# Joining the two head tiles in the second mix, and re-timing softmax, spare banks and fillers around both ends of a two-mix kernel

## The chip, the cores and the metric

One NeuronCore of a Trainium2 chip runs the whole program. The metric is device microseconds of one execution; lower is better. The profile's times count from the span's start.

## The reference

Three layers follow each other over a batch of 2 sequences of 4160 tokens, 192 channels wide, in float32 (five of the weights arrive as float64):

```python
# 1. attention over a window of 7 tokens, 8 heads
w = softmax(weight_gen, axis=-1)                       # (2, 4160, 8, 7)
x = einsum('bshk,bskhg->bshg', w, windows(x_pad))      # token s sees s-6 .. s
# 2. first mix: token shift, squared ReLU, sigmoid gate
xk = mu_k * x + (1 - mu_k) * x_prev;  xr = mu_r * x + (1 - mu_r) * x_prev
x = sigmoid(xr @ w_r) * (maximum(xk @ w_k, 0)**2 @ w_v)        # hidden width 1024
# 3. second mix: ReLU, convolution over 3 tokens, gate
h = maximum(x @ w_in, 0)                                       # hidden width 1024
x = (h * sigmoid(conv3(h, conv_w))) @ w_out
```

## The kernel before

The tokens of each sequence are cut into ten tiles (SIZES, line 16): 256, 248, seven of 472, and 352. Channels lie on partitions in both mixes, tokens along the free dimension.

**Attention** (`attention`, line 401) runs on GpSimd. A tile's rows are loaded from DRAM by SyncE; a tile has 2, 4 or 3 slots of 128 tokens per batch, and each slot of each batch (a "token" call, line 409) is four GpSimd instructions on `prod`, the last of which writes `tok`. Softmax weights sit in `sw`. `softmax` (line 371) computes them in six steps: VectorE's maximum over the window, a subtraction (GpSimd, for tile 0 VectorE), ScalarE's Exp, VectorE's sum, VectorE's reciprocal, a multiplication (GpSimd). It is done for tiles 0, 1, 2, and for tiles 3 to 9 as seven blocks whose maxima and sums lie in `stage`.

**Mixing** (`mixing`, line 430) transposes `tok` on TensorE into a `pa` bank (flip) and forms the shifted blends. It has three units per tile: unit 0 is batch 0's first 128 channels, unit 1 is batch 1's, unit 2 the last 64 channels of both. A value is kept as a rounded part and a remainder (`hi`, `lo`), so each product takes several passes. The remainder is GpSimd's work (VectorE's for tile 0). Unit 2's results are spread by DMAs into `xB`.

**First mix** (`moe1`, line 528): for each tile i, batch b and chunk fi of 128 of the 1024 hidden columns, five matmuls into a `pa` bank (two of them), two ScalarE steps (Relu, Square), a ScalarE copy and a VectorE subtraction into a buffer `s` (two), then five matmuls into the accumulators `am` and `ar`. `gate_r` (line 510) makes the gate, `mix_out` (line 587) multiplies it in and writes the next layer's input `x2[b]`; `carry` (line 575) keeps the last two columns of the tile before.

**Second mix** (`moe2`, line 623): for the same i, b, fi, five matmuls into a `pc` bank (two of them), Relu into `h` (two), a scaled copy back to the bank, two taps of the convolution (VectorE, line 645), Sigmoid, a product, a copy and a subtraction into `g` (two), and five matmuls into the accumulators `bm` and `br`. `store` (line 681) writes the outputs.

**Weight preparation** (`prepare`, line 351; `narrow`, line 286): SyncE loads chunks of the float64 weights into three slots of `stage`; `narrow` rebuilds float32 in two PSUM tiles px and py with one ScalarE and five VectorE steps. px alternates between `bm` and `br`, py between the two `pc` banks (lines 254 and 255). `split` makes the rounded part and the remainder.

**The order.** Every step is put on a plan at a program time t by `at(t, ...)`: tile i's first mix starts at 16 i, batch 1's half at 16 i + 8, one unit per chunk; the second mix follows LAG = 10 units later. Buffers rotate in plan order (`Ring`). `Program.schedule` (line 99) then orders each engine's instructions: a list scheduler with hand-fitted durations (`cost`, line 72) starts, on whichever engine is free first, the ready instruction with the smallest t. A PSUM tile counts as one region whatever columns are named (line 68). The resulting order is fixed; on the chip each engine runs its list in order and waits for semaphores. A result becomes ready for others after a latency; between two TensorE instructions there is none:

```python
for j in succ[i]:
    ready[j] = max(ready[j], t + dur[i] if eng == "PE" == self.ops[j][0] else end)
```

All DMAs are issued by SyncE in one such list.

Of the kernel before, what the change touches and what calls it, by code (L numbers as in the profile page):

```python
# [8 lines left out]
F32R = mybir.dt.float32r  # L9
# [17 lines left out]
LAG = 10  # L27

# [5 lines left out]
class Program:  # L34
# [37 lines left out]
    def cost(self, eng, method, out, ins, pointer):  # L72
# [21 lines left out]
        if eng == "POOL":  # L94
            busy = 0.1 + (n / 455 if method == "tensor_tensor" else n / 270)
            return busy, busy + 0.12
        return 0.6, 0.6

    def schedule(self):
# [42 lines left out]
        for _ in range(n):  # L142
# [22 lines left out]
        for i in sorted(range(n), key=lambda i: (start[i], i)):  # L165
            eng, method, a, k = self.ops[i][:4]
            getattr(self.real[eng], method)(*a, **k)  # L167
# [14 lines left out]
def conv_moe_kernel(ctx: ExitStack, tc: tile.TileContext, xp, wg_first, wg_rest, mus, w_k, w_v, w_r, w_in, conv_w, w_out, out):  # L182
# [18 lines left out]

    W = NMAX + 4

# [167 lines left out]
    def softmax(j, a, b, eng, times, bank):  # L371
# [19 lines left out]
        for t, fn in zip(times, (lambda: fold(m, ALU.max), lambda: each(m, ALU.subtract), s3,  # L391
                                 lambda: fold(z, ALU.add), s5, lambda: each(m, ALU.mult))):
            at(t, fn)
# [36 lines left out]
    def mixing(i, u, t, dt_):  # L430
        N, P, e = SIZES[i], PART[i], EXTRA[i]
        c = 1 if u == 2 else 0
        st = {}

        def flip():
            p = pa_r()
            st["p"] = p[:, e:e + N]
            st["q"] = p
            x = tok_t[i]
            k = (0, 256, 128)[u]  # L440
            for l in range(SLOTS[i]):
                PE.transpose(p[:, l:l + SLOTS[i] * (P - 1) + 1:SLOTS[i]], x[:, l, k:k + 128], ident)

        def shifted(fn):
            a = att_r()[:, :N]
            if e:
                fn(a, st["q"][:, e - 1:e + N - 1])
            else:
                POOL.memset(a[:, 0:1], 0.0)
                fn(a[:, 1:N], st["q"][:, 0:N - 1])  # L450
# [6 lines left out]
        def m1(k):  # L457
# [3 lines left out]
            if i < 2:  # L461
                a = shifted(lambda y, x: ACT.activation(y, x, ACTF.Copy, scale=onemu[:, own]))
                DVE.scalar_tensor_tensor(out=st[k][:, :N], in0=st["p"], scalar=mu[:, own], in1=a, op0=ALU.mult, op1=ALU.add)
            else:
                DVE.scalar_tensor_tensor(out=st[k][:, :N], in0=st["d"], scalar=onemu[:, own],
                                         in1=st["p"], op0=ALU.mult, op1=ALU.add)

        def hi(k):
# [6 lines left out]
            ACT.copy(x[:, 0, :N], st[k][:, :N])  # L475
# [351 lines left out]
```

## Time and profile before

| | us |
|---|---|
| median of 3 runs | 791.23 |
| lowest, highest | 789.27, 791.41 |
| profiled execution | 793.36 |
| its span | 791.6 |

Busy shares of the span: TensorE 88%, ScalarE 84%, VectorE 80%, GpSimd 64%. A share is an average over stretches with different limits; the rows below cut the span into stretches and then look at single engines. PE is TensorE's matmuls, PEld its weight loads, DVE VectorE, ACT ScalarE, POOL GpSimd, SP SyncE. Each row of a timeline gives start, duration, engine, line, operation, out<-in, shape and count; in square brackets stands the idle time before it and what ended it. Line 167 is the planner's call that issues everything.

### The profile page before, as it was taken

The numbers are of one execution on the slowest core, as the hardware profiler recorded it, in microseconds if no ns is written. First come the engines' busy times: TensorE is split into PE (matmuls) and PEld (weight loads), VectorE is DVE, ScalarE is ACT, GpSimd is POOL, SyncE is SP. The second block draws the span as 40 slices with busy tenths as digits, with TensorE's granted clock in tenths as the row PEclk, the third lists the DMA queues.
The fourth block names the chain that finished last, engine by engine and source line by source line (L and its number), as shares of the span: only waits on it lengthen the run. The fifth ranks groups of instructions, "written<-read, shape, count | busy, mean of one in ns | idle before, by whom it ended". The sixth has DMA issues, their size and how long they took to land.

```text
span 791.6 us, 10781 instructions
## 1 busy us (share of the span) xinstructions
PE 697.2 (88%) x3505; PEld 607.3 (77%) x3505; DVE 631.4 (80%) x1137; ACT 666.5 (84%) x1441; POOL 506.2 (64%) x368
## 2 busy tenths in 40 slices
PE   0066776999999999999999999999999999999964
PEld 0054675898888888888888888888888888889843
DVE  5987977887878787878877887879787878788764
ACT  2467798998989899989898989989898989899854
POOL 5898888899999999999999789295401101000000
PEclk9997786999999999999999999999999999999998
DMA  7685010130130112112121211020002000100000
GB/s 202 194 277 174 13 51 11 58 103 10 61 99 19 51 69 59 59 51 91 28 69 51 68 46 58 7 68 1 20 12 56 20 1 21 35 19 1 20 14 14
DMA packets 19241, 45.09 MB, mean 57 GB/s; under 512 B 3057, under 2 KB 14705, under 8 KB 19057
## 3 DMA queue, kind: packets, MB, share of 16 engines
q1 hardware_dynamic: 19184, 44.41, 18.9%
q8 instruction: 27, 0.44, 0.2%
q14 instruction: 30, 0.24, 0.1%
HBM read 27.40 MB, written 6.39 MB: 43 GB/s over the span
## 4 chain that ended last, share of the span: by engine, by line
PE 68%; ACT 15%; DVE 13%; issue 2%; DMA 2%; SPq 0%; ACTq 0%; DVEq 0%
PE pa L167 21%; PE pc L167 16%; PE am L167 10%; PE bm L167 9%; PE ar L167 7%; PE br L167 5%; DVE pc L167 4%; ACT pa L167 2%; ACT pc L167 2%; DVE stage L167 2%; ACT h L167 2%; ACT g L167 2%; ACT L167 1%; DMA stage<-in_moe_w_k_dram 1%; DVE bm L167 1%
## 5 line engine op out<-in xcount | busy, mean ns | idle before, releaser
L167 DVE SCALAR_TENSOR_TENSOR pc<-h,cw,pc 128x472 f32<-128x472 f32 (+3 forms) x320 | 208.1, 650 | 39.5 <-ACT pc L167 36.7
L167 POOL TENSOR_TENSOR prod<-rows,sw 128x1344 f32<-128x1344 f32 x70 | 216.1, 3087 | 12.8 <-DMA rows<-in_x_dram 7.8
L167 ACT ACTIVATE pa<-pa 128x472 f32<-128x472 f32 (+3 forms) x320 | 160.8, 505 | 39.1 <-PE pa L167 35.2
L167 POOL TENSOR_TENSOR prod<-prod 128x576 f32<-128x576 f32 (+1 forms) x140 | 171.0, 1221 | 8.6
L167 PE MATMUL bm<-g,wo 128*128 128x472 f32 (+3 forms) x480 | 148.7, 360 | 21.3 <-ACT g L167 21.1
L167 PE MATMUL am<-s,wv 128*128 128x472 f32 (+3 forms) x480 | 147.0, 367 | 7.1 <-ACT s L167 5.8
L167 DVE TENSOR_TENSOR pc<-h,pc 128x472 f32<-128x472 f32 (+3 forms) x160 | 94.7, 592 | 59.2 <-ACT pc L167 57.9
L167 PE MATMUL pa<-xA,wkA 128*128 128x472 f32 (+3 forms) x480 | 125.9, 368 | 7.5 <-DVE s L167 3.4
L167 PE MATMUL pc<-x,wiA 128*128 128x474 f32 (+3 forms) x480 | 121.6, 361 | 3.5 <-DVE g L167 3.5
L167 POOL TENSOR_TENSOR xA<-mk,xA 128x472 fp32r<-128x472 f32 (+2 forms) x36 | 40.4, 1128 | 123.1 <-ACT xA L167 96.6
L167 PE MATMUL ar<-s,wv 128*128 128x472 f32 (+3 forms) x320 | 112.6, 364 | 4.9 <-DVE x L167 3.3
L167 PEld LDWEIGHTS bm<-g,wo 128*128 128x128 f32 x480 | 88.3, 191 | 35.4 <-ACT g L167 26.0
L167 PE MATMUL br<-g,wo 128*128 128x472 f32 (+3 forms) x320 | 112.4, 355 | 1.4 <-DVE ob L167 1.4
L167 DVE TENSOR_TENSOR s<-pa,s 128x472 fp32r<-128x472 f32 (+3 forms) x160 | 93.7, 586 | 16.8 <-ACT s L167 15.8
L167 DVE TENSOR_TENSOR g<-pc,g 128x472 fp32r<-128x472 f32 (+3 forms) x160 | 93.8, 586 | 15.5 <-ACT g L167 14.0
L167 PEld LDWEIGHTS am<-s,wv 128*128 128x128 f32 x480 | 89.1, 197 | 21.4 <-ACT s L167 11.0
L167 PEld LDWEIGHTS pa<-xA,wkA 128*128 128x128 f32 x480 | 87.6, 199 | 19.9 <-DVE s L167 6.4
L167 ACT ACTIVATE pc<-h,cw 128x472 f32<-128x472 f32 (+3 forms) x160 | 99.7, 623 | 1.8
L167 PEld LDWEIGHTS pc<-x,wiA 128*128 128x128 f32 x480 | 85.7, 193 | 15.9 <-DVE g L167 5.8
L167 ACT ACTIVATE h<-pc 128x474 f32<-128x474 f32 (+3 forms) x160 | 84.4, 527 | 11.4 <-PE pc L167 8.3
L167 ACT ACTIVATE pc<-pc 128x472 f32<-128x472 f32 (+3 forms) x160 | 80.9, 506 | 14.0 <-DVE pc L167 13.0
L167 PE MATMUL pa<-xB,wkB 128*128 128x472 f32 (+3 forms) x320 | 89.8, 362 | 1.5 <-DMA xB<-mk 1.5
(105 smaller groups left out, 1066.4 us busy)
## 6 DMA issues: line engine op xcount, KB each, us to landing
rows<-in_x_dram SPq DMA_DIRECT2D x14, 960.0 KB, 4.5
xB<-rm SPq DMA_DIRECT2D x28, 118.0 KB, 2.3
xB<-mk SPq DMA_DIRECT2D x28, 118.0 KB, 2.3
out_dram<-om SPq DMA_DIRECT2D x14, 236.0 KB, 2.0
rows<-in_x_dram SPq DMA_DIRECT2D x4, 768.0 KB, 7.1
rows<-in_x_dram SPq DMA_DIRECT2D x2, 864.0 KB, 4.5
out_dram<-ob SPq DMA_DIRECT2D x14, 118.0 KB, 2.2
stage<-in_moe_w_v_dram SPq DMA_DIRECT2D x4, 384.0 KB, 3.9
```

Of the source, the lines that this page charges most:

```text
L167: getattr(self.real[eng], method)(*a, **k)
```

## The change

What it does, part by part:

- SIZES become 256, 220, seven of 476, 352. The first mix keeps ten tiles. In the second mix tiles 0 and 1 are one unit of 476 columns: `moe2` and `store` are planned for i >= 1 only, at tile 1's times, over `x2` columns that `mix_out` of both tiles has filled (OFFSET, UNIT).
- The planner treats a GpSimd result as ready for GpSimd when the instruction ends (as for TensorE), and its GpSimd durations change by 0.05 us.
- Softmax of tiles 3 to 9 moves from program times 16.5 to 25 (and 24.9 + 16 j for the last step) to 32.1 to 40 (and 36.1 + 12.5 j). Its seven Exps become one over all seven blocks, at 35.2. Its load may not be issued before planned time 50 us (40 before). Attention of tile 3 moves later by 2.4 (load) and 3.2 units.
- Weight preparation of the second mix moves from program times 4.4 to 10 to 6 to 18. px is `bm` alone, py `br` alone.
- Spare buffers are lent. Until program time 24 `moe1` and flips rotate over `pa` and `pc` banks, and `s` over `s` and `g` buffers. From 160.3 on `moe2` rotates over `pc` and `pa` banks, `h` over `h` and `mk`, `g` over `g` and `s`.
- Fillers: matmuls of 248 columns on a constant tile `spare`, into columns 264 to 511 of the `am` bank, which no one reads. The planner puts them in front of TensorE instructions before which it sees a gap over 0.3 us, until the first matmul that covers those columns (tile 2's). Within 9 us before the first matmul a gap gets 0.88 gap / 0.225 of them, later 0.65 gap / 0.12.
- First loads: SyncE issues tile 0's rows of batch 0, then `sw`, then `mu` (before: `mu`, `sw`, rows). A VectorE memset fills `spare`.
- A flip issues its transposes with the last slot first. (The diff also lets `mixing` take units 3 and 4; none is planned.)

```diff
-SIZES = [256, 248] + [472] * 7 + [352]
+SIZES = [256, 220] + [476] * 7 + [352]
+OFFSET = [0, SIZES[0]] + [0] * (NTILE - 2)
+UNIT = [None, SIZES[0] + SIZES[1]] + SIZES[2:]
+DONE = 16 * NTILE + 0.3
+LENT = 24
...
             for j in succ[i]:
-                ready[j] = max(ready[j], t + dur[i] if eng == "PE" == self.ops[j][0] else end)
+                ready[j] = max(ready[j], t + dur[i] if eng in ("PE", "POOL") and eng == self.ops[j][0] else end)
...
+            if eng == "PE":
+                idle &= not self.covers(a[0])
+                gap = start[i] - max(last, first - 9.0)
+                if idle and gap > 0.3:
+                    cold = start[i] <= first
+                    for _ in range(int((0.88 if cold else 0.65) * gap / (0.225 if cold else 0.12))):
+                        self.filler()
+                last = start[i] + dur[i]
             getattr(self.real[eng], method)(*a, **k)
...
+    class Shift:
+        def __init__(self, own, lent, till=None, since=None):
+            self.both, self.own, self.tiles, self.till, self.since = Ring(own + lent), Ring(own), own, till, since
+        def __call__(self):
+            if self.since is None:
+                return self.both() if prog.now < self.till else self.own()
+            if prog.now < self.since:
+                return self.own()
...
+            return self.both()
...
-    s_r = ring("s", 2, [128, 2, NMAX], F32R)
+    s_r = Shift(ring("s", 2, [128, 2, NMAX], F32R).tiles, g_r.tiles, till=LENT)
...
-    pa_r = Ring([bank(f"pa{j}") for j in range(2)])
+    pa_r = Shift([bank(f"pa{j}") for j in range(2)], pc_r.tiles, till=LENT)
-    px_r = Ring([bm_r.tiles[0], br_r.tiles[0]])
-    py_r = Ring(pc_r.tiles)
+    aside = am_r.tiles[0][:, 264:512]
+    def filler():
+        nc.tensor.matmul(aside, lhsT=spare[:, 0:128], rhs=spare, start=not begun, stop=False, skip_group_check=True)
+        begun.append(1)
+    px_r, py_r = bm_r, br_r
+    pt_r = Shift(pc_r.tiles, pa_r.tiles, since=DONE)
+    ht_r = Shift(h_r.tiles, mk_r.tiles, since=DONE)
+    gt_r = Shift(g_r.tiles, s_r.tiles, since=DONE)
...
-    softmax_load(3, wg_rest[:, (slots[1] + slots[2]) * KH:], 10.2, 40.0)
+    softmax_load(3, wg_rest[:, (slots[1] + slots[2]) * KH:], 18.2, 50.0)
...
-        softmax(3, a, b, POOL, (16.5 + 0.3 * j, 16.6 + 0.3 * j, 19.5 + 0.1 * j, 20.5 + 0.5 * j, 20.6 + 0.5 * j, 24.9 + 16 * j), None)
+        softmax(3, a, b, POOL, (32.1 + 0.4 * j, 32.15 + 0.4 * j, None, 35.3 + 0.8 * j, 35.4 + 0.8 * j, 36.1 + 12.5 * j), None)
+    at(35.2, lambda: ACT.activation(sm[3][0], sm[3][0], ACTF.Exp))
...
-                moe2(i, b, fi, t + fi + LAG)
+                if i:
+                    moe2(i, b, fi, t + fi + LAG)
```

## Rows read from the trace of the kernel before

**Rows 1.** The page, part 1: busy us (share of the span) and instructions
```profile
PE 697.2 (88%) x3505; PEld 607.3 (77%) x3505; DVE 631.4 (80%) x1137; ACT 666.5 (84%) x1441; POOL 506.2 (64%) x368
```

**Rows 2.** Busy time by stretch (us from the span's start), all engines
```profile
core 0: us, PE busy (x) PEld busy (x) DVE busy (x) ACT busy (x) POOL busy (x), PEclk, DMA share, GB/s
0.00:166.40 166.40, 95.27 (x571) 85.69 (x572) 133.77 (x295) 114.72 (x294) 140.85 (x116) 0.89 0.41 121
166.40:233.20 66.80, 66.03 (x369) 58.01 (x368) 52.24 (x104) 60.40 (x145) 63.98 (x45) 1.00 0.22 64
233.20:700.00 466.80, 463.97 (x2191) 401.24 (x2190) 380.83 (x619) 424.43 (x854) 299.92 (x207) 1.00 0.14 42
700.00:749.00 49.00, 48.43 (x268) 44.55 (x268) 38.56 (x70) 44.40 (x102) 1.50 (x3) 1.00 0.05 16
749.00:791.60 42.60, 23.54 (x114) 17.84 (x112) 25.97 (x51) 22.52 (x50) 0.00 (x0) 0.94 0.04 13
```

**Rows 3.** Timeline of TensorE, two stretches of tile 0's second batch
```profile
83.97 0.41 PE L167 MATMUL ar<-s,wv 128*128 128x256 f32 x1
84.19 0.41 PE L167 MATMUL am<-s,wv 128*128 128x256 f32 x1
...
90.67 0.28 PE L167 MATMUL am<-s,wv 128*128 128x256 f32 x1
90.79 0.28 PE L167 MATMUL ar<-s,wv 128*128 128x256 f32 x1
```

**Rows 4.** Timeline of TensorE, tile 2's last transposes and its first matmuls
```profile
157.20 0.63 PE L167 MATMUL pa<-ident,tok 128*128 128x128 f32 x4 [1.19 <-DVE mk L167]
...
165.99 0.73 PE L167 MATMUL pa<-xA,wkA 128*128 128x472 f32 x4
```

**Rows 5.** Timeline of GpSimd: its first product, tok of tiles 0, 2, 3
```profile
9.14 3.01 POOL L167 TENSOR_TENSOR prod<-rows,sw 128x1344 f32<-128x1344 f32 x1 [7.76 <-DMA rows<-in_x_dram]
...
38.75 0.59 POOL L167 TENSOR_TENSOR tok<-prod 128x192 f32<-128x192 f32 x1
...
142.97 0.60 POOL L167 TENSOR_TENSOR tok<-prod 128x192 f32<-128x192 f32 x1
...
149.42 0.60 POOL L167 TENSOR_TENSOR tok<-prod 128x192 f32<-128x192 f32 x1
...
202.62 0.60 POOL L167 TENSOR_TENSOR tok<-prod 128x192 f32<-128x192 f32 x1
```

**Rows 6.** VectorE, ScalarE, GpSimd: busy time on stage, 85 to 140 us
```profile
85.00:140.00 55.00, 21.20 (x30) 0.00 (x0) 15.33 (x14) 0.80 0.06 22
```

**Rows 7.** Groups of ScalarE's instructions from 85 to 140 us
```profile
L167 ACT ACT_TABLE_LOAD x12 | 15.4, 1283 | 0.2
...
L167 ACT ACTIVATE sw<-sw 128x448 f32<-128x448 f32 x6 | 3.5, 578 | 0.1
```

**Rows 8.** Timeline of ScalarE, first and last Relu of the tail
```profile
750.77 0.47 ACT L167 ACTIVATE h<-pc 128x356 f32<-128x356 f32 x1 [0.28 <-PE pc L167]
...
781.66 0.47 ACT L167 ACTIVATE h<-pc 128x356 f32<-128x356 f32 x1 [0.19 <-PE pc L167]
```

**Rows 9.** Groups of VectorE's instructions by shape, taps of the second mix
```profile
L167 DVE SCALAR_TENSOR_TENSOR pc<-h,cw,pc 128x472 f32<-128x472 f32 x224 | 158.8, 709 | 28.3 <-ACT pc L167 26.1
...
L167 DVE SCALAR_TENSOR_TENSOR pc<-h,cw,pc 128x256 f32<-128x256 f32 x32 | 15.4, 480 | 2.3 <-ACT pc L167 2.2
```

**Rows 10.** Timeline of VectorE, ends of the softmax chain of tile 0
```profile
4.92 0.55 DVE L167 TENSOR_REDUCE smz<-sw 128x32 f32<-128x224 f32 x1 [2.37 <-DMA sw<-in_first_dram]
...
7.89 0.39 DVE L167 TENSOR_TENSOR sw<-sw,smz 128x224 f32<-128x224 f32 x1
```

**Rows 11.** Timeline of VectorE, start of the tail, back to back
```profile
749.48 0.53 DVE L167 TENSOR_TENSOR am<-r,am 128x352 f32<-128x352 f32 x1
749.91 0.58 DVE L167 SCALAR_TENSOR_TENSOR pc<-h,cw,pc 128x354 f32<-128x354 f32 x1
750.41 0.52 DVE L167 TENSOR_TENSOR ar<-r,ar 128x352 f32<-128x352 f32 x1
```

More of the change, by code (lines that the diff above doesn't have):

```diff
@@ L94, in cost @@
         if eng == "POOL":
-            busy = 0.1 + (n / 455 if method == "tensor_tensor" else n / 270)
-            return busy, busy + 0.12
+            busy = 0.15 + (n / 455 if method == "tensor_tensor" else n / 270)
+            return busy, busy + 0.1
         return 0.6, 0.6
@@ L164, in schedule @@
                     open_[self.ops[j][0]].append(j)
-        for i in sorted(range(n), key=lambda i: (start[i], i)):
+        order = sorted(range(n), key=lambda i: (start[i], i))
+        first = next(start[i] for i in order if self.ops[i][1] == "matmul")
+        idle, last = True, 0.0
+        for i in order:
             eng, method, a, k = self.ops[i][:4]
+            if eng == "PE":
[6 more added lines that the diff above has]
+                last = start[i] + dur[i]
             getattr(self.real[eng], method)(*a, **k)
@@ L202, in conv_moe_kernel @@
     W = NMAX + 4
+    spare = new("spare", [128, 248], F32R)
+    class Shift:
[6 more added lines that the diff above has]
+                return self.own()
+            if not self.both.n:
+                k = self.own.n % len(self.tiles)
+                self.both.tiles = self.tiles[k:] + self.tiles[:k] + self.both.tiles[len(self.tiles):]
+            return self.both()
     mu = new("mu", [128, 4])
@@ L392, in softmax @@
                                  lambda: fold(z, ALU.add), s5, lambda: each(m, ALU.mult))):
-            at(t, fn)
+            if t is not None:
+                at(t, fn)
     rows_t, tok_t = {}, {}
@@ L436, in flip @@
             p = pa_r()
-            st["p"] = p[:, e:e + N]
+            st["p"] = p[O, e:e + N]
             st["q"] = p
             x = tok_t[i]
-            k = (0, 256, 128)[u]
-            for l in range(SLOTS[i]):
-                PE.transpose(p[:, l:l + SLOTS[i] * (P - 1) + 1:SLOTS[i]], x[:, l, k:k + 128], ident)
+            k, n = ((0, 128), (256, 128), (128, 128), (128, 64), (128, 128))[u]
+            for l in reversed(range(SLOTS[i])):
+                PE.transpose(p[0:n, l:l + SLOTS[i] * (P - 1) + 1:SLOTS[i]], x[:, l, k:k + n], ident)
         def shifted(fn):
-            a = att_r()[:, :N]
+            a = att_r()[O, :N]
             if e:
-                fn(a, st["q"][:, e - 1:e + N - 1])
+                fn(a, st["q"][O, e - 1:e + N - 1])
             else:
                 POOL.memset(a[:, 0:1], 0.0)
-                fn(a[:, 1:N], st["q"][:, 0:N - 1])
+                fn(a[:, 1:N], st["q"][O, 0:N - 1])
             return a
@@ L487, in lo @@
                     SP.dma_start(out=f(z[own, :N]), in_=f(x[own, 0, :N]))
-                    SP.dma_start(out=f(z[oth, :N]), in_=f(y[own]))
+                    SP.dma_start(out=f(z[oth, :N]), in_=f(y[own] if u == 2 else y))
         at(t, flip)
@@ L624, in moe2 @@
         last = i == NTILE - 1
-        N = SIZES[i] + (2 if last else 0)
+        N = UNIT[i] + (2 if last else 0)
         X = x2[b]
@@ L681, in store @@
     def store(i, b, t):
-        N = SIZES[i]
+        N = UNIT[i]
         last = i == NTILE - 1
-        a = 1 if i == 0 else 0
+        a = 1 if i == 1 else 0
         n = N + (1 if last else 0)
-        t0 = STARTS[i] - 1
+        t0 = STARTS[i] - OFFSET[i] - 1
         st = {}
@@ L712, in identity @@
     def identity():
+        DVE.memset(f(spare), 1.0)
         POOL.memset(ident, 0.0)
```

53 lines of the change are left out of this document (30 added, 23 removed).

## The prediction

> **What bounds the kernel now.** I read the page first, then the table of stretches, then timelines of single engines. By the page TensorE is busy for 88% of the span [rows 1]. An average hides where the rest is, so the table by stretch comes next [rows 2]. From 233 to 700 us TensorE is busy 464.0 of 466.8 us at full clock: only fewer columns would help there, and the change keeps their number. Before 166.4 us it is busy for 95 of 166, at a mean clock of 0.89, and after 749 us for 23.5 of 42.6. The two ends are where time lies.
>
> To price them I need the speed of useful work. Matmuls of 256 columns start 0.12 us apart at full clock (2.4 GHz) and 0.22 at half (1.2 GHz) [rows 3]; with 472 columns it is 466.8/2191 = 0.213 [rows 2]. I call "lost" the time gone minus the matmuls started at their full-clock spacing. The 571 matmuls before 166.4 us [rows 2] are 20 transposes and 551 of 248 to 258 columns (nearly all): 551 x 0.12 + 20 x 0.11 = 68.3 us. So 166.4 - 68.3 = 98.1 us are lost when tile 2 begins its first mix at 165.99 [rows 4]. From there to 749 us TensorE idles only 4.2 us more. The end loses 42.6 - 114 x 0.16 = 24 (0.16 for 356 columns, between the two spacings).
>
> In the **head** GpSimd sets the pace: one token row takes 6.45 us from tok to tok [rows 5], 16 of them are due before both batches of tile 2 are there, and the mixed unit of tile 2 needs both. It begins at 9.14 us, has tile 0's four at 39.34 and tile 2's last at 143.57 [rows 5]. Between those it ran 12 tokens (77.4 us) and 15.33 us of softmax for tiles 3 to 9, which no one needs yet; that softmax also took 21.2 us of VectorE [rows 6] and brought ScalarE 12 table loads, 15.4 us [rows 7]. VectorE is the second bound, busy 133.8 of 166.4 us [rows 2]. In the **tail** two pc banks set the pace: each chunk of 128 columns of the hidden width starts with a Relu into h, and nine steps lie between the Relu at 750.77 and that at 781.66, 3.43 us each [rows 8].
>
> **The change, part by part.**
>
> *Tile sizes and joined head tiles.* Columns stay 4160 per pass and batch. Seven tiles gain 4 columns: 7 x 340 matmuls x 4 x (0.213 - 0.12)/216 us = 4.1 us. Tile 1 falls from 248 to 220; bounds are 0 (a floor) and 180 x 28 x 0.093/216 = 2.2 us; I take 1. In the second mix a pair of 256 and 248 becomes one of 476, 16 times: 10 x (0.12 + 0.12 - 0.213) x 16 = 4.3 us. Net for TensorE about 0. VectorE and ScalarE lose 64 instructions each; a tap costs 480 ns at 256 columns and 709 at 472 [rows 9], so joining two saves about 0.23 us, 14 us on each engine, all in the head.
>
> *GpSimd's order.* The planner now treats a GpSimd result as ready for GpSimd at once, so other softmax no longer slips between tokens. The first four tokens took 30.2 us, of which 4 x 6.45 = 25.8 are theirs; 4.4 us move behind them. Tile 0 is ready some 4 us sooner, tile 1 not.
>
> *First loads.* SyncE now issues rows, then sw, then mu. GpSimd's start waited for rows [rows 5], and the softmax chain from sw's landing ran from 4.92 to 8.28 us [rows 10]. Rows may land 0.9 us sooner; sw, now behind 768 KB, may land 1 to 2 us later and end the wait instead. Bounds -0.9 and +1.5; I take +0.5.
>
> *Softmax postponed.* 15.3 us of GpSimd leave the stretch before tile 2's last token: 143.6 - 15.3 + 0.5 = about 129. From a flip to the first matmul took 165.99 - 157.20 = 8.8 us [rows 4], so tile 2 can begin at about 138 instead of 166. VectorE allows it: 133.8 - 21.2 (softmax) - 19 x 1.8 (chunks of the small tiles' second mix, two taps and two shorter ones each) + 8 x 2.7 (the joined one) = 100 us of work in 138. Useful TensorE work by then: first mix of tiles 0 and 1, 360 x 0.12 = 43.2; joined second mix of batch 0, 80 x 0.213 = 17.0; transposes 2.2; two or three us of batch 1: 65. Lost: 138 - 65 = 73, against 98.1: the head gains 25 us.
>
> What comes back: the postponed work now falls into tile 2's stretch, where TensorE is full. VectorE is busy 380.8/466.8 = 82% there [rows 2], so it has 13 us free in 73 us of a tile, and gets 14 to 21: 1 to 8 us late. The single Exp covers 54 x 56 = 3024 columns; 448 took 0.578 us [rows 7], so it takes 2.8 to 3.9, with two table loads a block of 6 us on ScalarE, against two pa banks of prepared work (2.1 us): some 3 us of TensorE. GpSimd needs 8/14 of 15.3 = 8.8 us and a wait for Exp (about 5) before tile 3's tokens; their last then ends at 129 + (203.2 - 143.6) + 14 = 203, as before [rows 5]. Second-mix work fills that wait at first, but alone it runs at the two-bank pace. I take 5 us in all as paid, between 1 and 18: head net 20.
>
> *Spare banks at the start, weight preparation with one px and one py.* Four pa banks let four matmul groups run ahead; worth 0 beyond the above, since tokens pace. One px bank stops the next chunk's ScalarE step from overlapping the last one's split: up to about 2 us for each of 16 chunks, 30 us of delay on that chain, none at least. VectorE has other work meanwhile, and the second mix's weights are not read before tile 1's first mix of batch 0 is done: 0. Without that cover a few us, which the range holds.
>
> *Fillers.* GpSimd paces the stretch they run in, so a warm clock is worth 0 to 3 us; I take 0. Where they run in real idle time they cost nothing. The memset of their operand and the reversed order of transposes cost nothing: the last token releases a flip either way. The planner's own rule counts any two accesses of one PSUM bank as dependent, and fillers write am.
> The Trainium skill (PSUM — Partial Sum Buffer, Terms) speaks against such lending: two engines at once on one bank and quadrant are an error, so fillers have to wait for VectorE's and ScalarE's steps on am, which would lead to the slower rival below; no run here shows it yet.
>
> *Spare banks at the end.* From program time 160.3 on, batch 0's chunks 6 and 7 and all of batch 1's get four banks, four h and four g. One bank's turn took 2 x 3.43 = 6.9 us, so four allow 1.7 us; VectorE's four instructions start 0.43 and 0.50 us apart when back to back [rows 11], 1.86 us in all; TensorE needs 10 x 0.16. The pace becomes 1.9 to 2.9 us, the latter if the written-out order keeps engines waiting; I take 2.2. Nine steps: 9 x (3.43 - 2.2) = 11 us, bounds 5 and 14. What is late next there is VectorE.
>
> **Sum.** 20 + 11 = 31 us. The profiled execution took 793.4 us (span 791.6), 2.1 above the median of 791.2: 793.4 - 31 = 762.4, as a median about 760.
>
> **Rivals.**
> - *The postponed softmax is paid in full* (0.24): it meets a full VectorE and late tokens of tile 3; 18 instead of 5 come back, head 7: 773. For it: VectorE's 82%. Against: second-mix work is queued to fill TensorE.
> - *Better than that* (0.15): nothing comes back and the tail reaches VectorE's pace, 25 + 14: 752, or 744 if the half-clock stretches lay on the path too.
> - *The tail keeps its pace* (0.07): lent banks change nothing because the written order couples the chunks; 771. Here the change would not do what it says. Against: each bank's next matmul waits on that bank's own last step.
> - *Slower, by fillers* (0.06): the fillers stand behind a wait instead of within it. Some 33 us of planned gaps between tile 0's tokens and tile 2 (138 less 40, less 65 of work) give 33 x 0.65/0.12 = 179 fillers; where a gap ends by a step on am, its fillers wait for that step too and then stand before the matmul. At half clock, 0.21 us each: 38 us against 31 gained, 798. It decides from about 150 such fillers on. Against: other engines touch am only in tile 0's mixing and at four ends of a first mix.
>
> **Numbers.** The forecast has 0.46, with its own range 752 to 769. The rest, 0.02, is no change. Range: 744 to 778, which takes in the first three rivals and the bounds of what comes back. Faster by over 0.3% (about what a measurement of this kernel can tell from none): 0.92; same 0.02; slower 0.06.
>
> **What would show it.** Right: tile 2's last tok at 125 to 133 us with no stage softmax before it; its first matmul near 138; one Exp between two table loads during tile 2; Relu to Relu near 2.2 us in the tail; TensorE full between. Wrong: tokens on time but tile 2 beginning after 150 (VectorE or fillers pace the head); TensorE gaps of over 15 us in all between tile 2 and tile 4; Relu steps still above 3 us.

## The result and the profile after

The change takes the median from 791.1 to **780.7 us** (780.1 to 782.8), a ratio of 0.988 with a 95% interval of 0.9863 to 0.9897. 760 was forecast, with a range of 744 to 778: the sign was right, the size a third of the 31 us forecast. The profiled execution of the change took 780.3 us (span 778.5), that of before 793.4, so the two traces differ by 13.1 us and the medians by 10.4.

The page of the kernel after, part 1 (busy time, share of the span, instructions), answers [rows 1]:

```profile
PE 719.1 (92%) x3573; PEld 617.9 (79%) x3573; DVE 623.1 (80%) x1072; ACT 644.4 (83%) x1355; POOL 507.5 (65%) x368
```

TensorE's 92% contain 228 fillers. They count as busy and compute nothing, so the row overstates what was won.

Busy time by stretch of the kernel after, cut at 138 us, where the prediction had tile 2 begin, at 220 us, where the postponed work is over but for GpSimd's multiplications, and around the tail; columns as in [rows 2]:

```profile
0.00:138.00 138.00, 102.32 (x676) 92.38 (x676) 108.06 (x223) 81.17 (x219) 113.24 (x95) 0.91 0.45 140
138.00:220.00 82.00, 75.64 (x334) 62.63 (x333) 67.78 (x114) 70.34 (x134) 67.07 (x47) 0.96 0.16 47
220.00:700.00 480.00, 474.01 (x2206) 403.15 (x2205) 385.80 (x622) 430.24 (x859) 327.12 (x227) 1.00 0.15 43
700.00:746.00 46.00, 45.45 (x251) 41.92 (x251) 36.58 (x66) 41.73 (x96) 0.11 (x1) 1.00 0.06 17
746.00:778.50 32.50, 21.64 (x113) 17.83 (x111) 24.84 (x51) 20.88 (x50) 0.00 (x0) 0.91 0.06 17
```

The second row is the news: TensorE idles over 6 us there, at a clock of 0.96, where [rows 2] showed a full engine from tile 2's start on. And by 138 us VectorE was busy for 108.06 us; the prediction had counted 100. Part of the postponed work never left the head. VectorE's timeline after, first and last of the seven maxima of tiles 3 to 9:

```profile
114.76 1.00 DVE L186 TENSOR_REDUCE stage<-sw 128x64 f32<-128x448 f32 x1
...
125.62 0.77 DVE L186 TENSOR_REDUCE stage<-sw 128x48 f32<-128x336 f32 x1
```

The plan has them at program times 32.1 to 34.5, behind tile 2's start, but the planner starts whatever is ready on a free engine, so they run before tile 2 begins: 6.7 us of VectorE.

GpSimd's timeline after, which answers [rows 5]: first product, tile 0's last tok, the wait behind it, tile 1's first tok, tile 2's last, the wait for the postponed softmax, tile 3's last:

```profile
10.93 3.07 POOL L186 TENSOR_TENSOR prod<-rows,sw 128x1344 f32<-128x1344 f32 x1 [9.52 <-DVE sw L186]
...
35.75 0.59 POOL L186 TENSOR_TENSOR tok<-prod 128x192 f32<-128x192 f32 x1
...
49.42 1.16 POOL L186 TENSOR_TENSOR sw<-sw,smz 128x448 f32<-128x448 f32 x1 [3.52 <-DVE smz L186]
53.12 0.60 POOL L186 TENSOR_TENSOR tok<-prod 128x192 f32<-128x192 f32 x1
...
128.46 0.60 POOL L186 TENSOR_TENSOR tok<-prod 128x192 f32<-128x192 f32 x1
...
155.32 1.16 POOL L186 TENSOR_TENSOR sw<-sw,stage 128x448 f32<-128x448 f32 x1 [12.42 <-DVE stage L186]
...
209.72 0.59 POOL L186 TENSOR_TENSOR tok<-prod 128x192 f32<-128x192 f32 x1
```

TensorE's timeline after, tile 2's last transposes and its first matmuls, which answers [rows 4]:

```profile
131.47 0.60 PE L186 MATMUL pa<-ident,tok 128*128 128x128 f32 x4
...
133.63 0.81 PE L186 MATMUL pa<-xA,wkA 128*128 128x476 f32 x3
```

ScalarE's timeline after, first and last Relu of the last ten chunks, which answers [rows 8]:

```profile
747.50 0.47 ACT L186 ACTIVATE h<-pc 128x356 f32<-128x356 f32 x1 [0.27 <-PE pc L186]
...
768.45 0.47 ACT L186 ACTIVATE h<-pc 128x356 f32<-128x356 f32 x1
```

So tile 2 begins 32 us sooner than before, and the tail's step is 20.95/9 = 2.33 us instead of 3.43. Both came about as forecast, and only one of them is in the time. To see where the other went I follow **lost time** through the run, as the prediction did, with a spacing for each width (a lower quartile of the starts that follow each other: 0.107 us at 128 columns, 0.1175 at 256, 0.2135 at 472, 0.2155 at 476, 0.161 at 356; fillers count as nothing). By these, all useful matmuls take 653.3 us before and 654.6 after. "end" is the span minus that.

```
lost by (us)                           80    140    160    220    340    380    740    end
before                               65.7   96.0   99.6  102.6  104.6  105.7  113.6  138.3
lending at the end alone (x17)       64.7   93.3   97.1  100.0  102.0  103.1  111.2  125.3
after                                60.2   80.3   88.0   91.9   94.6   99.2  109.2  123.9
```

At 140 us the change is 13.0 us ahead of the second line. By 220 us 8.1 of them are left, at 380 us 3.9 and at 740 us 2.0, with 1.3 us more work to do.

Each line is one execution. The first two have the same order of work up to the tail, and yet differ by 2.5 us at 160 us; so a difference of 2 or 3 us between two lines, here and in the table below, is a hint and no more.

### The profile page after: what moved, and what is told of

It is laid out like the page before. It is cut to its first block, busy times and chain, and to the rows that moved or that the text cites. A ratio compares the mean times of both kernels' runs of the same rounds, so it can differ in the third digit from the quotient of the medians.

```text
span 778.5 us, 10731 instructions
## 1 busy us (share of the span) xinstructions
PE 719.1 (92%) x3573; PEld 617.9 (79%) x3573; DVE 623.1 (80%) x1072; ACT 644.4 (83%) x1355; POOL 507.5 (65%) x368
## 4 chain that ended last, share of the span: by engine, by line
PE 52%; POOL 15%; DVE 15%; ACT 12%; issue 3%; DMA 2%; SPq 0%; ACTq 0%; DVEq 0%; POOLq 0%
PE pa L186 15%; PE pc L186 13%; POOL prod L186 12%; PE am L186 8%; PE bm L186 6%; PE ar L186 5%; DVE pc L186 4%; PE br L186 4%; ACT pa L186 2%; ACT pc L186 2%; DVE bm L186 2%; DVE stage L186 2%; PE am L298 1%; ACT h L186 1%; POOL tok L186 1%
## 5 line engine op out<-in xcount | busy, mean ns | idle before, releaser
L186 DVE SCALAR_TENSOR_TENSOR pc<-h,cw,pc 128x476 f32<-128x476 f32 (+1 forms) x280 | 196.8, 703 | 36.3 <-ACT pc L186 33.8
L186 ACT ACTIVATE pa<-pa 128x476 f32<-128x476 f32 (+4 forms) x298 | 153.1, 517 | 35.1 <-PE pa L186 31.4
L186 PE MATMUL bm<-g,wo 128*128 128x476 f32 (+1 forms) x417 | 137.3, 376 | 6.1 <-ACT g L186 5.8
L186 PE MATMUL am<-s,wv 128*128 128x476 f32 (+3 forms) x444 | 137.7, 367 | 3.3 <-ACT s L186 3.3
L186 DVE TENSOR_TENSOR pc<-h,pc 128x476 f32<-128x476 f32 (+1 forms) x140 | 90.1, 643 | 49.2 <-ACT pc L186 47.6
L186 PE MATMUL pc<-x,wiA 128*128 128x478 f32 (+1 forms) x420 | 115.4, 380 | 1.5 <-DVE g L186 1.4
L186 PE MATMUL pa<-xA,wkA 128*128 128x476 f32 (+3 forms) x441 | 113.7, 363 | 1.8 <-DVE s L186 1.7
L186 PE MATMUL ar<-s,wv 128*128 128x476 f32 (+3 forms) x296 | 104.3, 365 | 2.9 <-ACT x L186 2.8
L186 PE MATMUL br<-g,wo 128*128 128x476 f32 (+1 forms) x278 | 104.7, 378 | 0.2 <-ACT xA L186 0.2
L186 DVE TENSOR_TENSOR s<-pa,s 128x476 fp32r<-128x476 f32 (+4 forms) x142 | 86.6, 611 | 11.8 <-ACT s L186 11.6
L186 ACT ACTIVATE pc<-pc 128x476 f32<-128x476 f32 (+3 forms) x166 | 86.1, 519 | 10.8 <-DVE pc L186 7.0
L186 ACT ACTIVATE pc<-h,cw 128x476 f32<-128x476 f32 (+1 forms) x140 | 92.6, 662 | 1.6
```

## The experiments

All were timed beside runs of the kernel before on the same chip. The change itself is the first line.

```
label                   median us   ratio to before (95%)     lost by 160   220    380    end
(the change)               780.73   0.9880 (0.9863-0.9897)          88.0   91.9   99.2  123.9
x2_no_lending              790.14   0.9995 (0.9979-1.0011)          87.6   91.0   98.1  133.2
x17_lending_alone          781.18   0.9884 (0.9863-0.9904)          97.1  100.0  103.1  125.3
x3_no_late_softmax         772.89   0.9776 (0.9760-0.9793)          79.4   81.1   92.3  116.3
x7_no_late_exp             777.81   0.9838 (0.9821-0.9855)          86.3   90.2   95.3  121.3
x4_split_softmax           780.50   0.9876 (0.9856-0.9895)          83.9   92.5   99.0  124.0
x16_spread_sums            780.65   0.9871 (0.9856-0.9885)          89.9   94.3   98.1  124.4
x6_early_softmax           790.19   0.9986 (0.9970-1.0002)          99.6  102.3  107.2  131.9
x5_old_pool_rule           784.00   0.9917 (0.9900-0.9934)          94.4   98.4  102.2  127.4
x12_pool_order             781.36   0.9882 (0.9864-0.9899)          88.4   93.0  100.0  124.7
x14_less_vector            772.82   0.9773 (0.9759-0.9788)          79.8   82.6   92.1  115.8
x15_less_gpsimd            777.10   0.9823 (0.9808-0.9838)          85.4   91.0   95.3  119.0
x8_dve_softmax             780.50   0.9877 (0.9855-0.9899)          92.5   93.6   99.2  123.6
x10_early_low              784.75   0.9936 (0.9918-0.9955)          95.7   97.5  103.3  127.9
x11_all                    780.99   0.9875 (0.9855-0.9895)          95.5   97.1  100.9  125.3
x1_no_fillers              781.22   0.9880 (0.9864-0.9897)          88.4   94.1  101.1  125.8
x9_third_mk                778.74   0.9853 (0.9833-0.9873)          88.4   92.3   96.6  122.1
x13_mk_and_fillers         781.10   0.9875 (0.9860-0.9890)          91.0   95.6   99.4  125.3
x18_best                   774.53   0.9783 (0.9759-0.9806)          84.1   89.5   94.0  118.1
```

### The tail, taken out and alone

```diff
-DONE = 16 * NTILE + 0.3
+DONE = 16 * NTILE + 1000.0
```

> The change without the banks, h and g lent at the end; everything before about 735 us keeps its order. Theory (two banks set the pace of the tail): Relu to Relu in the last chunks goes back to 3.3 to 3.5 us from 2.33, and the time is 789 to 792 us. Rival (the tail is shorter because less work is left for it, not because of the lent banks): 781 to 784 us.

790.1 us: the lending is worth 790.1 - 780.7 = 9.4, and without it the change can't be told from the kernel before. ScalarE's timeline in this run, first and last of the last ten Relu:

```profile
746.50 0.47 ACT L186 ACTIVATE h<-pc 128x356 f32<-128x356 f32 x1 [0.27 <-PE pc L186]
...
777.39 0.47 ACT L186 ACTIVATE h<-pc 128x356 f32<-128x356 f32 x1 [0.20 <-PE pc L186]
```

30.89/9 = 3.43 us a step, to the hundredth what [rows 8] had. The reverse is the kernel before with that one part:

```diff
+    pt_r = Shift(pc_r.tiles, pa_r.tiles, since=DONE)
+    ht_r = Shift(h_r.tiles, mk_r.tiles, since=DONE)
+    gt_r = Shift(g_r.tiles, s_r.tiles, since=DONE)
...
-            p = pc_r()
+            p = pt_r()
...
-            h = h_r()
+            h = ht_r()
...
-            g = g_r()
+            g = gt_r()
```

> The kernel before with one part of the change alone: the banks, h and g lent at the end. Theory (leaving this part out of the change cost all of its 10 us, so everything done to the head nets about zero): 780 to 783 us, as fast as the whole change, with Relu steps of 2.3 to 2.5 us in the last chunks. Rival (the head's earlier start and the lending only count together): 785 to 789 us.

781.2 us, the time of the whole change. ScalarE's timeline in this run, the same two Relu:

```profile
748.22 0.47 ACT L169 ACTIVATE h<-pc 128x356 f32<-128x356 f32 x1 [0.27 <-PE pc L169]
...
769.16 0.47 ACT L169 ACTIVATE h<-pc 128x356 f32<-128x356 f32 x1
```

2.33 us a step again. The two runs close the account from both sides: three lines of lending make the gain, and everything done to the head nets about zero. From 747.5 to 768.5 us of the kernel after, VectorE is busy for 20.05 of 21 us: with four banks it is the engine that is nearly full, as forecast.

### The postponed softmax

What the block does where it stands, in the kernel after: ScalarE, VectorE and TensorE between 142 and 157 us (start, duration; in brackets the idle time before it and what ended it):

```profile
144.14 0.62 ACT L186 ACTIVATE h<-pc 128x478 f32<-128x478 f32 x1
144.78 1.28 ACT L186 ACT_TABLE_LOAD   x1
146.07 2.73 ACT L186 ACTIVATE sw<-sw 128x3024 f32<-128x3024 f32 x1
148.71 0.55 ACT L186 ACTIVATE pa<-pa 128x476 f32<-128x476 f32 x1
149.19 0.55 ACT L186 CAST g<-pc 128x476 fp32r<-128x476 f32 x1
...
148.84 1.86 DVE L186 TENSOR_REDUCE stage<-sw 128x64 f32<-128x448 f32 x2 [3.66 <-ACT sw L186]
...
149.79 0.71 PE L186 MATMUL bm<-g,wo 128*128 128x476 f32 x2 [2.38 <-ACT g L186]
```

Read it from the last line back. TensorE waits 2.38 us for a g that ScalarE makes only after table load and Exp; VectorE meanwhile stands 3.66 us before a sum that needs the Exp, since its written order has the sum first. The stretches after such gaps run at a lower granted clock, in the kernel after:

```profile
151.00:155.00 4.00, 3.69 (x10) 3.10 (x11) 4.00 (x9) 0.95 (x3) 0.00 (x0) 0.57 0.01 4
...
161.00:165.00 4.00, 3.20 (x9) 2.71 (x9) 4.00 (x8) 2.19 (x5) 3.84 (x5) 0.59 0.07 15
```

```diff
-    for j in range(NTILE - 3):
-        a, b = (sum(slots[3:3 + k]) for k in (j, j + 1))
-        softmax(3, a, b, POOL, (32.1 + 0.4 * j, 32.15 + 0.4 * j, None, 35.3 + 0.8 * j, 35.4 + 0.8 * j, 36.1 + 12.5 * j), None)
-    at(35.2, lambda: ACT.activation(sm[3][0], sm[3][0], ACTF.Exp))
```

> Leaves out the softmax of tiles 3 to 9 (their weights are used as they were loaded), so no Exp, no table loads and no VectorE or GpSimd steps for it after 131 us. Theory (this block, on a VectorE and a ScalarE that are full, takes back about 10 us of the head's gain between 140 and 200 us): the time lost between 140 and 200 us falls from 11 to under 4 us, the half-clock stretches at 151 and 161 us go, and the time is 766 to 772 us. Rival (second-mix work left over from the head fills VectorE there in any case): 777 to 781 us with gaps of TensorE in the same place.

772.9 us, 7.8 less and 0.9 above the theory's range; the time lost from 140 to 220 us falls from 11.6 to 3.6. The full price is nearer to the 10.8 us that this run is ahead at 220 us: at 350 us it meets the wait described further down, in a worse form (a gap of 4.68 us). Of the 10.8 us, 2.8 are lost by 140 us, where the maxima run (a hint, by one trace each). The rival falls: without the block little is lost there.

```diff
-    at(35.2, lambda: ACT.activation(sm[3][0], sm[3][0], ACTF.Exp))
```

> Leaves out the one Exp over tiles 3 to 9 with its two table loads; VectorE and GpSimd still do all their steps of the block. If ScalarE's 5.3 us are what TensorE pays for in the block, the time falls by most of the 8 us that leaving out the whole block saved: 773 to 776 us. If it is VectorE's 12 us or GpSimd's wait for them: 778 to 781 us.

777.8 us, between the two. By 220 us this run is only 1.7 us ahead, of the block's 10.8; the rest of its 2.9 us it gains at 360 us, where it loses 1.4 instead of 4.6. So VectorE's and GpSimd's steps, which this run keeps, are the larger part of the block: some 9 us.

```diff
-        softmax(3, a, b, POOL, (32.1 + 0.4 * j, 32.15 + 0.4 * j, None, 35.3 + 0.8 * j, 35.4 + 0.8 * j, 36.1 + 12.5 * j), None)
-    at(35.2, lambda: ACT.activation(sm[3][0], sm[3][0], ACTF.Exp))
+        softmax(3, a, b, POOL, (32.1, 32.15, 32.2, 32.3, 32.4, 36.1) if j == 0 else (45.1 + 0.1 * j, 45.15 + 0.1 * j, None, 46.1 + 0.3 * j, 46.2 + 0.3 * j, 32.7 + 16 * j), None)
+    at(46.0, lambda: ACT.activation(sm[3][0][:, slots[3]:], sm[3][0][:, slots[3]:], ACTF.Exp))
```

> Only tile 3's softmax is done before tile 3's tokens; that of tiles 4 to 9 with one Exp of their own after them, near 200 us. Theory (the size of the one block is what hurts, and GpSimd's wait for it): tile 3's last token ends at 196 to 203 us instead of 210, gaps of TensorE between 140 and 170 us fall from 5.5 to under 3 us, and the second block costs 1 to 4 us later: 774 to 780 us. Rival (any block costs two table loads and the Exp wherever it stands, and two cost more than one): 781 to 786 us.

780.5 us, no gain, though the lost time moved as the theory had it: 85.5 at 200 us against 91.3. Then comes the second block (ScalarE's timeline in this run):

```profile
200.93 1.28 ACT L186 ACT_TABLE_LOAD   x1
202.23 2.35 ACT L186 ACTIVATE sw<-sw 128x2576 f32<-128x2576 f32 x1
204.60 1.28 ACT L186 ACT_TABLE_LOAD   x1
```

By 220 us the lost time is 92.5: the block of six tiles costs 7 us at 200 us too. It is dear in both places, where TensorE is full. The next run was to move only VectorE's sums away from the Exp (with a third mk buffer and the fillers; in the softmax line three of its times):

```diff
-35.3 + 0.8 * j, 35.4 + 0.8 * j, 36.1 + 12.5 * j
+35.3 if j == 0 else 32.5 + 12.5 * j, 35.4 if j == 0 else 32.6 + 12.5 * j, 36.1 + 12.5 * j
```

> The change with a third mk buffer, and the sums and reciprocals of tiles 4 to 9 each shortly before the tile that needs them instead of after the Exp. Theory (half of the block's 8 us is VectorE's work in a stretch where it is full): 774 to 777 us, with 1 to 4 us less lost from 140 to 180 us. Rival (the waits there are for the Exp and GpSimd's subtractions, not for the sums): as with the third mk alone, 777 to 779 us.

780.65 us; its measure is the kernel with a third mk and fillers, 781.10 (x13, further down). But the edit moved nothing. VectorE's timeline in this run, first and last of the sums:

```profile
149.79 1.81 DVE L186 TENSOR_REDUCE stage<-sw 128x64 f32<-128x448 f32 x2 [3.76 <-ACT sw L186]
...
176.20 0.83 DVE L186 TENSOR_REDUCE stage<-sw 128x48 f32<-128x336 f32 x1
```

In x13 they start from 151.09 to 177.49 us, and VectorE's order is the same from end to end: the planner put the sums into the same free slots, whatever their later times. The run is a repeat of x13 and leaves the theory untested. Which of VectorE's and GpSimd's steps make the block so dear stays open. Undoing the postponement altogether (the former softmax, load and chunk times; its plan is otherwise that of the change):

> The change with the softmax of tiles 3 to 9, its load and the weight chunks at their former times, an Exp per tile again. Theory (postponing moved the cost more than it saved it): tile 2's first matmul falls from 134 to 145 to 150 us, but TensorE loses under 4 us between 150 and 200 us, and the time is 779 to 786 us: postponing is worth 0 to 5 us. Rival (postponing is what the head's gain rests on): 791 us and above.

790.2 us: postponing is worth 9.5 us, more than the theory had and just short of the rival. In this run TensorE's useful work is no further at 160 us than in the kernel before (99.6 lost in both).

### Who paces the head

The prediction took GpSimd to pace the head, and VectorE to allow it. First the order on GpSimd alone, the softmax of tiles 1 and 2 between tokens again (of each line the part that differs):

```diff
-POOL, (-82.6, -82.5, -82.4, -82.35, -82.3, -82.25), ar_r
+POOL, (-89.95, -83.65, -83.64, -83.63, -83.62, -82.25), ar_r
...
-softmax(2, 0, slots[2], POOL, (0.9, 0.91, 0.92, 0.93, 0.94, 0.95), None)
+softmax(2, 0, slots[2], POOL, (0.9, 2.2, 2.25, 2.3, 2.35, 16.9), None)
```

> The change with the softmax of tile 1 put between tile 0's tokens again, and that of tile 2 between tile 1's and tile 2's, so that GpSimd never waits for VectorE between 36 and 53 us. Theory A (GpSimd paces the head): tile 1's first token ends near 46 us instead of 53.7, tile 2's last near 121 instead of 129, and the time falls by 4 us or more, to 772 to 777 us. Theory B (VectorE paces the head from there on, and the tokens only wait in line): the tokens are as early, but the time lost at 160 us stays within 3 us of 88, and the time is 778 to 782 us.

781.4 us, the time of theory B, with 88.4 us lost at 160 us. But only the tokens of tile 1 end sooner, by 9.4 us, and then GpSimd stands (its timeline in this run):

```profile
63.02 0.60 POOL L186 TENSOR_TENSOR tok<-prod 128x192 f32<-128x192 f32 x1
71.28 1.27 POOL L186 TENSOR_TENSOR xA<-mk,xA 128x220 fp32r<-128x220 f32 x2 [7.66 <-ACT xA L186]
```

The wait of 7.66 us for tile 1's mixing takes back most of the 9.4 us won; tile 2's last token ends at 129.9, against 129.1 without the edit. So this run shows that the order of softmax and tokens isn't what counts; what earlier tokens of tile 2 would bring it can't tell. Then work was taken from one engine at a time:

```diff
-        DVE.tensor_scalar(y, x, 0xFF800000, None, op0=ALU.bitwise_and)
-        DVE.scalar_tensor_tensor(out=f(z), in0=lo, scalar=2.0 ** -52, in1=py, op0=ALU.mult, op1=ALU.mult)
-        DVE.tensor_tensor(px, px, f(z), op=ALU.add)
```

> Leaves out three of VectorE's five steps that turn a weight chunk into fp32 (the low words are dropped), some 30 us of VectorE before 140 us; nothing of GpSimd's. If VectorE paces the head from tile 1 on, the time lost at 160 us falls from 88 to under 81 us, and the time to 766 to 774 us. If GpSimd does, the time lost at 160 us stays at 85 to 90 us, and the time at 778 to 782 us.

```diff
-            eng.tensor_tensor(y[:, 0:3], y[:, 0:3], y[:, 3:6], op=ALU.add)
-            eng.tensor_tensor(y[:, 0:2], y[:, 0:2], y[:, 2:7:4], op=ALU.add)
```

> Leaves out two of GpSimd's additions in each token row (two taps of seven are used), which takes a token from 6.4 to about 3.8 us; nothing of VectorE's. If GpSimd paces the head, the time lost at 160 us falls from 88 to under 78 us, and the time to 755 to 768 us. If VectorE does, tile 2's last token comes 30 us or more sooner, but the time lost at 160 us only falls to 82 to 87 us; the gap at 360 us goes also: 770 to 777 us.

Busy time from 40 to 140 us, columns as in [rows 2], for the kernel after:

```profile
40.00:140.00 100.00, 87.25 (x590) 77.99 (x591) 85.18 (x181) 72.84 (x202) 88.41 (x68) 0.95 0.37 116
```

with less of VectorE (x14):

```profile
40.00:140.00 100.00, 89.96 (x598) 80.08 (x599) 71.25 (x140) 74.30 (x205) 90.64 (x69) 0.97 0.35 107
```

and with less of GpSimd (x15):

```profile
40.00:140.00 100.00, 85.88 (x579) 75.47 (x578) 87.67 (x180) 77.57 (x201) 61.46 (x43) 0.98 0.41 127
```

The steps left out in x14 take 623.1 - 599.5 = 23.6 us off VectorE's busy time over the run, and 14 off the 85 in this stretch, as other work comes sooner. The lost time at 160 us falls by 8.2, and the run takes 772.8. With 27 us less of GpSimd's 88, tile 2's last tok ends at 87.4 us instead of 129.1, 42 us sooner, and the lost time at 160 us falls by 2.6; most of that run's 3.6 us come from the wait at 360 us, which it doesn't have. So the weights' and VectorE's side sets the head far more than the tokens do. x14 also shortens the chain of steps of each weight chunk, whose px and py banks the change made single; the run doesn't tell that chain's length from VectorE's occupation. The reverse, more of VectorE early, speaks for occupation: the softmax of tiles 3 to 9 on VectorE with one Exp before 80 us,

> A version meant to be faster: the softmax of tiles 3 to 9 with a buffer of its own, loaded by about 25 us and done on VectorE (its subtractions too) with one Exp before 80 us, where VectorE has 4 to 7 us free in each 20; only the last multiplications stay on GpSimd; no fillers (to make room). Theory (the block costs 8 us because it stands where VectorE and ScalarE are full, and costs little earlier): 771 to 776 us, with under 4 us lost from 140 to 200 us. Rival (VectorE also paces the head, so its 12 us come back there in full): 780 to 788 us, tile 2 starting after 138 us with as much lost by then as is saved later.

gave 780.5 us, no gain over the change (10 us more lost by 80 us, all but 1.7 of them given back by 220), and the same planned behind the first mix's weights,

> As the version with the softmax of tiles 3 to 9 early on VectorE, but behind the weights of the first mix (maximum, subtraction and Exp in 50 to 90 us; sums and reciprocals spread over the tiles that follow), no fillers. Theory (done before those weights it starved TensorE from 60 to 80 us, 10 us, which ate what it saved later): the time lost by 80 us is under 63 us again, under 93 at 180 us, and the time is 772 to 777 us. Rival (VectorE has no free time before 140 us anywhere): 779 to 783 us.

784.75 us, above both ranges, with 67.4 lost by 80 us where under 63 was expected. In its trace the maxima run from 34.8 us, the Exp at 63.8 and the sums from 66.6 to 97.2: sooner than meant, and the sums are not spread. Where the block ran, VectorE had no room either; the place that was meant is tried only in part. With x12's order and a third mk buffer added,

> The three together: third mk buffer, early softmax of tiles 3 to 9 behind the first weights, GpSimd's order in the head, no fillers. If each does what its theory says, 764 to 772 us; if VectorE paces the head whatever the order, 776 to 780 us (the gap at 360 us alone).

781.0 us, above both ranges too: not what the sum of the theories said, and with the block as early as in x10. Last, the planner's former rule and constants for GpSimd:

```diff
-                ready[j] = max(ready[j], t + dur[i] if eng in ("PE", "POOL") and eng == self.ops[j][0] else end)
+                ready[j] = max(ready[j], t + dur[i] if eng == "PE" == self.ops[j][0] else end)
...
-            busy = 0.15 + (n / 455 if method == "tensor_tensor" else n / 270)
-            return busy, busy + 0.1
+            busy = 0.1 + (n / 455 if method == "tensor_tensor" else n / 270)
+            return busy, busy + 0.12
```

> The change with the planner's former rule and constants for GpSimd (a result counts as ready for GpSimd itself only at its end; 0.1 and 0.12 us), and nothing else undone. Theory (the new rule bought 3 us at tile 0 and cost more behind it): GpSimd's idle time from 36 to 50 us goes because softmax slips between the first tokens again, tile 1's first token ends at 45 to 48 us instead of 53.7, the 2-us gap of TensorE at 360 us goes, and the time is 774 to 779 us. Rival (the later tile 0 costs as much as that): 780 to 785 us.

784.0 us, the rival: the gap at 360 us went, but tile 0's last tok came at 41.6 and tile 2's at 138.3. The new rule is worth 3.3 us.

### The fillers

What they do in tile 0's mixing, in the kernel after (TensorE and ScalarE):

```profile
43.40 3.99 PE L298 MATMUL am<-spare 128*128 128x248 f32 x17 [6.34 <-DVE am L186]
...
47.42 0.37 ACT L186 CAST xA<-am 128x256 fp32r<-128x256 f32 x1 [3.58 <-PE am L298]
```

They wait for VectorE's step on am, and ScalarE's step on am waits for them: the mechanism of the slower rival. The Trainium skill (PSUM — Partial Sum Buffer, Terms) has two engines at once on one bank and quadrant as an error. No run here shows that error: the planner keeps all accesses of am apart, and in the trace no filler overlaps another engine's step on am. The price was measured:

```diff
-                if idle and gap > 0.3:
+                if False and gap > 0.3:
```

> The 228 filler matmuls are not issued; nothing else is changed. Theory (the fillers are worth little either way, the postponed softmax took the missing time): the granted clock falls in more stretches before 80 us, the waits of VectorE and ScalarE for fillers on am (3.6 and 2.1 us) go, and the time stays at 778 to 785 us. Rival (the fillers hold up tile 0's mixing and so cost part of the head): 772 to 777 us, with the first mix of tile 1 some 5 us sooner. Other rival (the warm clock is what brought the head's gain): 786 to 795 us.

781.2 against 780.7 us. Busy time by stretch without fillers,

```profile
40.00:80.00 40.00, 28.02 (x165) 25.12 (x166) 32.46 (x72) 29.89 (x87) 34.03 (x26) 0.91 0.57 178
80.00:140.00 60.00, 47.74 (x273) 41.35 (x272) 50.98 (x104) 40.24 (x110) 51.39 (x39) 0.89 0.21 65
```

and with them:

```profile
40.00:80.00 40.00, 33.46 (x229) 30.43 (x230) 31.04 (x69) 28.41 (x83) 32.84 (x26) 0.89 0.53 167
80.00:140.00 60.00, 53.79 (x363) 47.56 (x363) 54.14 (x112) 44.43 (x120) 55.57 (x43) 1.00 0.27 83
```

From 40 to 80 us the granted clock (PEclk) isn't lower without them, against what was expected; from 80 to 140 us it is 0.89 without them and 1.00 with them. By 80 us 0.9 us less are lost without them, by 140 us 2.1 us more; the medians differ by 0.5 us. So the net is worth next to nothing; the run doesn't part what the waits cost from what the clock gives.

### The wait at 360 us

GpSimd, VectorE, ScalarE and TensorE after, in order of time:

```profile
357.50 3.10 POOL L186 TENSOR_TENSOR prod<-rows,sw 128x1344 f32<-128x1344 f32 x1
...
360.56 1.19 POOL L186 TENSOR_TENSOR xA<-mk,xA 128x476 fp32r<-128x476 f32 x1
...
361.79 0.71 DVE L186 SCALAR_TENSOR_TENSOR mk<-att,onemu,pa 128x476 f32<-128x476 f32 x1 [2.34 <-POOL xA L186]
362.54 0.59 ACT L186 CAST rm<-mk 128x476 fp32r<-128x476 f32 x1 [2.05 <-DVE mk L186]
...
362.56 1.11 PE L186 MATMUL pa<-xA,wrA 128*128 128x476 f32 x3 [2.03 <-DVE mk L186]
```

A token's product was written ahead of the subtraction that frees mk; VectorE waits for that mk, ScalarE and TensorE behind VectorE. From 360 to 380 us 4.1 us are lost, against 0.6 in x9 below: the 2.03 us become 3.5. From 363 to 367 us the granted clock is 0.57, which makes up an estimated 4 x (1 - 0.57) = 1.7 us:

```profile
363.00:367.00 4.00, 4.00 (x13) 3.40 (x12) 2.29 (x5) 3.30 (x7) 3.92 (x5) 0.57 0.46 107
```

```diff
...
-    mk_r = ring("mk", 2, [128, NMAX])
+    mk_r = ring("mk", 3, [128, NMAX])
```

> The change with a third mk buffer and, to make room for it, no fillers (these alone gave 781.2 us). Theory (near 360 us VectorE stands before a mk that GpSimd has not yet subtracted from, since one of GpSimd's token products went first, and TensorE waits behind it): the 2-us gap of TensorE and the half clock after it go, and the time is 776 to 779 us. Rival (the next buffer in that chain makes the same wait): 780 to 782 us.

778.7 us; TensorE has no gap near 360 us, and from 360 to 380 us it loses 0.6 instead of 4.1. With the fillers back,

> The change with a third mk buffer and its fillers. Theory (the third mk took the gap at 360 us away, worth 2.5 us against the same kernel without fillers, and the fillers are worth half a us): 777 to 779 us. Rival (fillers cost): above 779 us.

781.1 us: the gap stays away, but by 220 us this run has lost 95.6 against 92.3. Such an edit gives the planner another order. Repeats of one order differ as well: x16, with the order of this run, has 94.3. Whether the fillers cost 2 us here is not shown.

### A version that beats both

> A version meant to beat both: the change with the low words of the weights dropped (30 us less of VectorE before 140 us), a third mk buffer, no fillers. Theory (the two gains add: 8 for VectorE, 2 to 2.5 for the gap behind mk): 768 to 772 us. Rival (the other order that a third mk gives the plan eats it): 772 to 776 us.

774.5 us (771.7 to 775.3), the rival's range: the third mk added nothing to x14, which took 772.8. Both use only the high word of each weight. Of the kernels that do all of the work, x9 is the fastest, 0.9853 (0.9833 to 0.9873) of the time before; that it beats the change itself, by 2.0 us, is less sure, as the two intervals overlap.

## Why the prediction was wrong, step by step

- **Tail: 11 us (5 to 14).** Right: 9.4 and 10.0 in the two runs; steps of 2.33 us for 2.2.
- **"GpSimd sets the pace", the premise of the head.** Wrong: in x15 tile 2's last tok ends 42 us sooner, and the lost time at 160 us falls by 2.6. The rows of before held a sign of it. Tile 2's last tok ends at 143.57 us [rows 5], and its last transposes begin at 157.20, behind a wait for VectorE [rows 4]. The step that put 8.8 us behind the last token left out these 13.6.
- **Tokens and tile 2's start.** The first date was right and the second 4 us off (129.06 for 129, 133.63 for 138), partly by luck: the first product came 1.8 us later than before, beyond the bound of 1.5, because it waited for the softmax behind sw's later landing; tile 0's tokens ended 3.0 us sooner instead of 4; tile 1's first came 17.4 us after tile 0's last, with two round trips through ScalarE and VectorE that the step "4.4 us move behind them" had left out.
- **"VectorE allows it", the step that failed first.** 65 us of useful TensorE work were expected by 138 us; the trace has 138 - 80.2 = 57.8. VectorE was busy 108 us by then, not 100. The sum took all 21.2 us of softmax out of the head, but the seven maxima, 6.7 us, still ran before tile 2; and 1.1 of the 21.2 are two steps of weight preparation, which use the stage buffer as well. Joining two instructions was counted as the difference of their durations, 0.23 us, but neighbours overlap ([rows 11]: 0.58 us long, the next one 0.50 later); over the run VectorE's busy time fell by 631.4 - 623.1 = 8.3 us, not 14. And a sum over 138 us counts idle time of the first 40 us, while loads arrive, as if it could be used later. In x14, where VectorE is busy for 92.6 us by 138 us, less than the 100 counted, the lost time there is 73.3, the 73 that was forecast. Measured in lost time between tile 2's starts, the head gained 97.3 - 78.6 = 18.7 us (x17 at 163.4, after at 133.6), not 25; against the trace of the kernel before, at 166.0, it is some 21.
- **What comes back: 5 us (1 to 18), the second failed step.** From tile 2's start to 220 us the change loses 13.3 us, x17 2.7: 10.6 come back. There is one Exp between two table loads, as forecast, and its parts were priced about rightly (1.28 us a load, Exp 2.73 for 2.8 to 3.9); so was its effect, some 3 us of TensorE (1.7 in x7). Tile 3's tokens ended at 210 instead of 203, but TensorE did not run dry of them. The term that was too small is VectorE's and GpSimd's: 1 to 8 us late, of which the total of 5 left some 2 as paid, where the runs show about 9 (10.8 in x3, less 1.7). Queued second-mix work was to cover them, but it needs the same ScalarE and VectorE: both gaps of TensorE, 2.38 and 1.75 us, are waits for a g of the second mix. And the half clock behind them was not priced: an estimated 4 x (0.43 + 0.41) = 3.4 us by the two rows above. The first rival, paid in full, named this mechanism, at 18 us.
- **Not foreseen:** the wait at 360 us, 3.5 us.
- **What is left:** 18.7 - 10.6 - 3.5 = 4.6. From 220 to 340 us 0.7 and from 380 to 740 us another 1.9 us go, in no gap that I could name (open), and 1.3 are added work of wider tiles and joined pairs, where 0 was forecast: 0.7 us for the head, as x2's 0.8.
- **Fillers 0:** right. **Spare banks at the start and single px and py, 0 each:** not tried alone. With the postponement undone the rest of the head's parts cost some 9 us (x6, against x17); of these only the planner's rule (a gain of 3.3) and the fillers were taken apart, so these two zeros are in doubt. Before 138 us VectorE waits 12 times, 6.5 us in all, for ScalarE's step on bm, where px is alone; in the kernel before it was 3 times, 4.7 us.

## What to carry to other kernels

When one engine's work is moved earlier, ask stretch by stretch what the others can do by then; a busy sum over the whole head hides that the early idle time is not theirs to use. A later time in a plan is not yet a later start: where the planner fills free slots, look in the trace for where the work went (the maxima here, and the sums in x16). Follow lost time to the end of the run before believing a gain at its start: here 19 us by 134 us were under 1 at the end. A bank's turn time in a drained tail, in contrast, is a serial chain that can be read off two rows and priced well.

## What the runs showed of the hardware

A short gap of TensorE can cost more than itself: after gaps of 2.38 and 1.75 us near 150 and 160 us, and of 2.03 us at 360 us, the granted clock fell to 0.57 to 0.59 over the 4 us read above, in part at half speed (1.2 GHz), and the 2.03 us at 360 us became 3.5. Not every gap did so: after one of 1.53 us, before 125.75 us in the same trace, the clock was 1.00 from 125.7 to 129.7 us. A warmer clock from 80 to 140 us (1.00 for 0.89, x1) came with 0.5 us in all, the fillers' own waits included; in that stretch other engines set the pace.
